# A transformer block on one Trainium2 core: another order for the lead-in's maxima, weight loads and low keys

## The chip, the cores and the metric

The kernel runs on one core of one Trainium2 chip. The metric is the device time of one execution in microseconds (us), as a median over runs. The profile shows one execution of its own. Engines: TensorE (PE; PEld is its weight load), VectorE (DVE), ScalarE (ACT), GpSimd (POOL) and SyncE (SP), whose queue issues nearly all DMA transfers, one after the other.

## What is computed

A layer norm, an attention in which 32 heads share one set of keys and values, and a feed-forward part with the Mish function, whose result passes through a silu and gates the attention's:

```python
B, S, D, H, F = 1, 2048, 512, 32, 1792        # head width Dh = 16
xn = layernorm(x)                              # x: [1, 2048, 512]
q  = (xn @ wq) split into 32 heads             # [32, 2048, 16]
k, v = xn @ wk, xn @ wv                        # [2048, 16] each, for all heads
p  = softmax(q @ k.T * Dh ** -0.5)
s  = (p @ v, heads joined) @ wo
h  = xn @ w1 + b1
g  = silu((h * tanh(softplus(h))) @ w2)
out = x + s * g
```

All of it is in float32; the products that need it are made of two parts, a rounded high part and the rest, the low part.

## The kernel before

The sequence is cut into four chunks of 512 rows, the heads into 32 units (`v`, 8 per chunk) of four heads. For every unit and each of 16 key blocks the main loop computes four tiles of scores (`e_one`, L1010), their exponential on ScalarE (L1015) and the value products (`pv`, L1097). The exponential needs each row's maximum first. So TensorE computes every score a second time the other way round (`m_one`, L1039), and VectorE reduces each 128 x 512 tile to 128 maxima (L1043): 64 tiles for a unit, 32 for each of two sides `a` of the partitions. The maxima run 22 steps (`LEAD`) ahead of the scores; `c_rows` turns a unit's maxima into rows and sends them into the query tile (L1082). Between these lie the projections of the feed-forward part and of the queries, as groups of 12 products into one bank `xps` (`fill`, L112 whole, L116 in halves beside other products). ScalarE empties a group's bank: `hb` (L763) for the first feed-forward layer, `qf` (L708) for queries.

Before the main loop stands the lead-in, at 0 to 99.5 us of the span: loading x, the norm, transposing x (`xp`, L294), the projection to keys and values (`kp`, L335), the first query group, and 88 of the tiles for the maxima: 64 of unit 0, and 12 of each side of unit 1.

- Keys. For chunk 0 the key rows come out on partitions 0 to 63 alone; for the others, half the columns on partitions 0 to 63 and half on 64 to 127. ScalarE copies the high parts to `ks` (`k_high`, L340), VectorE subtracts to the low parts (`k_low`, L169), and DMA carries each half to the other side (`k_move`, L348). A tile of maxima needs all 512 columns of its chunk on its side, so for chunk 0 only side 1 needs a transfer.
- Queries. `qt` (L722) takes 12 small transfers for each of units 0 and 1, in four parts of three: half `p` and side `a`.
- Values. ScalarE copies them out of the bank (`v_copy`, L353), TensorE transposes them (L358), VectorE copies them to `vaug` (L361).
- Weights. A weight block is loaded to one of two raw tiles (`rawws`, `rawwb`, `rawwq`; L495, L497). ScalarE writes its high part (L449), GpSimd its low part (L169); `xtw` and `ws` are such blocks of w1, `wbs` of w2. The raw tile is free for the next load once GpSimd has read it. An engine takes its instructions in order, and SyncE waits at a load until its raw tile is free.
- The order is found when the program is built: a planner in the lead-in has for each engine a list of tasks with estimated durations and picks the one that can start first (`best`, L1337). `m_ready` picks the next tile of the maxima, both sides as a pair; where nothing is ready, TensorE gets a group's products or a product that nobody reads (`keep_warm`, L1317). `landed` (L1202) estimates when a load has arrived, and `arrived` (L427) whether a block may be split.

In the main loop the order is written out by step: units of four steps, with the products of one group among them.

Of the kernel before, what the change touches and what calls it, by code (L numbers as in the profile page):

```python
# [20 lines left out]
P = 128  # L21
# [101 lines left out]
def block_kernel(ctx: ExitStack, tc: tile.TileContext, x, wq, wk, wv, wo, w1, b1, w2, out):  # L123
# [156 lines left out]
    def x_scale(t):  # L280
        x_ = xin[divmod(t, 4)]
        if t % 2 == 0:
            (dve if t < 4 else pool).tensor_scalar(x_, x_, rstd[:, t:t + 1], nbias[:, t:t + 1], op0=ALU.mult, op1=ALU.add)
        else:
            xn_scale(x_, x_, t)
# [64 lines left out]
    def v_copy(c):  # L350
        vt_of[c] = sb.tile([P, C], F32, tag="xr", name=f"vt{c}", bufs=4)[0:32]
        for o, z, _ in sides(c):
            act.activation(vt_of[c][:, z], kp_of[c][o + 32:o + 64, 0:z.stop - z.start], AF.Copy)  # L353

    def v_transpose(c):
        vp = vp_of[c] = ps_v.tile([P, 4, 32], F32, tag="v", name=f"vp{c}")
        for tt in range(4):
            pe.transpose(vp[:, tt], vt_of[c][:, P * tt:P * (tt + 1)], ident[0:32, 0:32])  # L358

    def v_out(c):  # L360
        dve.tensor_copy(vaug[:, 4 * c:4 * c + 4, 0:DH], vp_of[c][:, :, 16:32])  # L361
# [161 lines left out]
    def begin():  # L523
# [16 lines left out]
        else:  # L540
            ps = ps_x.tile([P, 512], F32, tag="x", name="xps")
# [154 lines left out]
    def q_group(c, b):  # L696
        it = item("wq", ("q", b), wq[:, P * b:P * (b + 1)].rearrange("(t p) n -> p t n", p=P))

        def post(ps):
# [12 lines left out]
            for k in range(2):  # L712
# [10 lines left out]
                if first:  # L723
                    lead["qdma"](lambda ps, dmas=dmas: dmas(parts=[(p, a) for p in ps for a in range(2)]))
# [460 lines left out]
    T = {"PE": 11.0, "ACT": 2.0, "DVE": 3.4, "POOL": 5.5, "SP": 3.0}  # L1185
# [16 lines left out]
    def landed(us):  # L1202
        dma_t[0] = max(dma_t[0] + us, now[0] + 2.2)
# [10 lines left out]
    def put_off(g, ps):  # L1214
# [4 lines left out]
        t = task("ACT", 0.69, fn, at=now[0] + 0.35)  # L1219
# [4 lines left out]
    def q_low(fn):  # L1224
        lead["qlow"] = task("DVE", 0.69, fn, at=T["ACT"] + 0.7)

    def q_dma(fn):
        v = len(qready)
        qready[v] = None

        def move(p):
            fn(ps=(p,))
            qready[v] = (qready[v] or ()) + (now[0] + 6 * 0.63 + 2.0,)
        for p in range(2):
            task("SP", 6 * 0.63, lambda p=p: move(p), [lead["moved"] if p + v else lead["qlow"]], prio=1 + p + 2 * v)
# [13 lines left out]
    xat.update({t: landed(DMA_US) for t in range(8, 16)})  # L1249
    warm = ps_v.tile([P, C], F32, tag="v", name="warm")  # L1250
# [12 lines left out]
    for t in range(12, 16):  # L1263
        ss = task("ACT", 0.6, lambda t=t: stats_sum(t), at=xat[t], prio=4)
        st.append(task("ACT", 0.6, lambda t=t: stats_var(t), [ss], prio=4))
    kv_done = None
    for c in range(NC):
# [6 lines left out]
        for t in range(4 * c, 4 * c + 4):  # L1274
            e, us = ("ACT", 0.8) if t % 2 else ("DVE", 0.55) if c == 0 else ("POOL", 0.8)
# [27 lines left out]
        kl = task("DVE", 0.86 if c else 0.68, lambda c=c: k_low(c), [kh])  # L1303

        def mv(c=c):
            k_move(c)
            kready[c] = now[0] + 2.6
# [3 lines left out]
        vc = task("ACT", 0.76 if c else 0.59, lambda c=c: v_copy(c), [kp])  # L1311
        bank("v", 1, k0, [kl, vc])
        vtr = task("PE", 0.5, lambda c=c: v_transpose(c), [vc], fill=c > 0)
        vo = task("DVE", 0.22, lambda c=c: v_out(c), [vtr])
# [9 lines left out]
    pick = [0]  # L1324

    def m_ready(t):
        if min(m_next) >= 2 * LEAD:
            return None
        s = [None, None]
        for v in range(2):  # L1330
            n = got[v]
            if n < 32 and len(qready.get(v) or ()) > n % 8 // 4 and n // 8 in kready:
                s[v] = max(t, qready[v][n % 8 // 4], kready[n // 8], m_ends[(-3, -5)[len(mseq) % 2] if 15 in xp_of else -2])
        pick[0] = int(s[0] is None or s[1] is not None and s[1] + 0.6 < s[0])
# [216 lines left out]
```

## Time and profile before

| | us |
|---|---|
| median of 3 runs (lowest, highest) | 1596.12 (1593.78, 1597.36) |
| the profiled execution | 1591.68 |
| its span, first to last instruction | 1589.9 |
| first product for maxima; first score | 29.19; 99.73 |
| TensorE busy in 110 to 200 us | 90.00 of 90 |
| TensorE busy in 20 to 100 us, eight windows of 10 | 8.21, 9.63, 5.98, 9.53, 9.21, 9.70, 7.03, 8.91 |

The profile has busy times per engine, windows of the span with the clock that TensorE was granted (1.00 is full), and timelines: start, length, engine, line, what was written from what, and in brackets how long the engine stood idle before it and what ended that. In a window the numbers after the length are busy us. Buffer numbers are left out there (`xtw<-rawws`), while the order of a program, below, keeps them (`rawws_537`).

### The profile page before, as it was taken

What the parts mean: (1) busy time and instruction counts of PE and PEld (TensorE: products, weight loads), DVE (VectorE), ACT (ScalarE), POOL (GpSimd) and SP (SyncE); (2) the same over time, 40 slices, a digit from 0 to 9 for tenths busy, and PEclk for the clock granted to TensorE, in tenths of its full rate; (3) what the DMA queues carried; (4) which work ended last, traced back from release to release, by engine and by line L of the source; (5) the groups of instructions that cost most, each with busy time, mean ns of one, the idle gap of its engine ahead of it and who ended that gap; (6) DMA issues with size and microseconds to landing.
All of it is one profiled execution on the core that took longest, in us unless ns stands there. A gap on an engine that the chain in (4) does not pass through costs nothing.

```text
span 1589.9 us, 31336 instructions
## 1 busy us (share of the span) xinstructions
PE 1567.2 (99%) x11680; PEld 881.2 (55%) x11680; DVE 1335.8 (84%) x2282; ACT 1297.4 (82%) x2512; POOL 638.9 (40%) x671
## 2 busy tenths in 40 slices
PE   8889999999999999999999999999999999999998
PEld 5445655655555565565555556556655555655643
DVE  6888888888988988888898988888889999888821
ACT  5469889878899778887988888797788978888796
POOL 4677438527368210531524523153152323315021
PEclk9899999999999999999999999999999999999999
DMA  6322125114152213103104230322321213031200
GB/s 185 122 90 87 31 74 164 58 53 158 33 177 63 77 58 111 57 24 104 55 18 150 65 104 26 102 69 70 110 58 49 88 58 115 15 97 32 74 21 27
DMA packets 74887, 124.42 MB, mean 78 GB/s; under 512 B 21536, under 2 KB 37184, under 8 KB 74736
## 3 DMA queue, kind: packets, MB, share of 16 engines
q1 hardware_dynamic: 74664, 122.41, 24.6%
q8 instruction: 93, 1.52, 0.4%
q14 instruction: 58, 0.48, 0.1%
q10 hardware_dynamic: 72, 0.01, 0.0%
HBM read 74.52 MB, written 26.21 MB: 63 GB/s over the span
## 4 chain that ended last, share of the span: by engine, by line
PE 94%; ACT 2%; DVE 1%; DMA 1%; POOL 1%; issue 0%; SPq 0%; DVEq 0%; POOLq 0%; ACTq 0%
PE xps L116 42%; PE pv L1097 31%; PE m L1039 11%; PE e L1010 6%; PE xps L112 1%; ACT pts L1015 1%; DVE mb L1043 1%; PE warm L1252 1%; PE warm L1321 0%; DMA rawwb<-in_dram 0%; PE wop L112 0%; PE xp L294 0%; SPq L722 0%; DMA rawws<-in_dram 0%; DMA rawwq<-in_dram 0%
## 5 line engine op out<-in xcount | busy, mean ns | idle before, releaser
L1043 DVE TENSOR_REDUCE mb<-m 128x1 f32<-128x512 f32 x2048 | 1266.2, 682 | 175.3 <-PE m L1039 152.5
L1015 ACT ACTIVATE pts<-e 128x512 f32<-128x512 f32 x2042 | 1062.4, 606 | 217.4 <-PE e L1010 147.3
L1039 PE MATMUL m<-ks,qt 48*128 48x512 f32 (+1 forms) x2048 | 842.4, 427 | 1.0 <-DMA ks<-ks 0.7
L1010 PE MATMUL e<-qt,ks 64*128 64x512 f32 x2048 | 747.2, 407 | 2.0 <-ACT pts L1015 1.7
L1097 PE MATMUL pv<-pts,vaug 128*32 128x512 f32 x4084 | 531.0, 603 | 0.0
L1039 PEld LDWEIGHTS m<-ks,qt 48*128 48x128 f32 (+1 forms) x2048 | 367.8, 186 | 106.4 <-DVE mb L1043 54.3
L1010 PEld LDWEIGHTS e<-qt,ks 64*128 64x128 f32 x2048 | 372.4, 186 | 28.6 <-ACT pts L1015 18.1
L116 PE MATMUL xps<-wbs,act 64*128 64x512 f32 x1248 | 315.2, 397 | 0.0
L116 PE MATMUL xps<-xt,ws 64*128 64x512 f32 x1122 | 311.4, 410 | 0.2 <-ACT pts L1015 0.2
L116 PEld LDWEIGHTS xps<-xt,ws 64*128 64x128 f32 x1122 | 193.3, 185 | 182.2 <-ACT pts L1015 121.3
L116 PEld LDWEIGHTS xps<-wbs,act 64*128 64x128 f32 x1248 | 226.5, 185 | 65.6 <-ACT pts L1015 33.5
L1097 PEld LDWEIGHTS pv<-pts,vaug 128*32 128x32 f32 x4084 | 87.8, 108 | 150.4 <-issue 142.4
L169 POOL TENSOR_TENSOR hb<-hb,t 128x512 f32<-128x512 f32 x56 | 72.2, 1289 | 152.7 <-ACT t L782 72.6
L179 POOL TENSOR_SCALAR t<-t 128x512 f32<-128x512 f32 x56 | 34.4, 615 | 171.6 <-ACT t L769 171.5
L116 PE MATMUL xps<-xt,wq 64*128 64x512 f32 x336 | 93.0, 409 | 0.0
L116 PEld LDWEIGHTS xps<-xt,wq 64*128 64x128 f32 x336 | 57.9, 185 | 55.0 <-ACT pts L1015 37.7
L169 POOL TENSOR_TENSOR oc<-oc,sc 128x512 f32<-128x512 f32 (+1 forms) x16 | 20.6, 1288 | 147.6 <-DMA qt<-qh 47.0
L116 PE MATMUL xps<-wbs,ot_all 64*128 64x512 f32 x288 | 79.4, 408 | 0.0
L116 PEld LDWEIGHTS xps<-wbs,ot_all 64*128 64x128 f32 x288 | 49.5, 184 | 47.1 <-ACT pts L1015 29.3
L169 POOL TENSOR_TENSOR act<-hb,act 128x512 fp32r<-128x512 f32 x56 | 72.2, 1290 | 4.7
L169 POOL TENSOR_TENSOR hb<-hb,u 128x512 f32<-128x512 f32 x56 | 72.3, 1291 | 4.4
L169 POOL TENSOR_TENSOR u<-u,t 128x512 f32<-128x512 f32 x56 | 72.0, 1285 | 4.7
(141 smaller groups left out, 885.9 us busy)
## 6 DMA issues: line engine op xcount, KB each, us to landing
wbs<-w SPq DMA_DIRECT2D x38, 512.0 KB
ws<-w SPq DMA_DIRECT2D x32, 512.0 KB
qt<-qh SPq DMA_DIRECT2D x256, 32.0 KB
w<-wbs SPq DMA_DIRECT2D x14, 512.0 KB
w<-ws SPq DMA_DIRECT2D x14, 512.0 KB
wq<-wq SPq DMA_DIRECT2D x14, 512.0 KB
rawws<-in_dram SPq DMA_DIRECT2D x24, 256.0 KB
wbs<-wo SPq DMA_DIRECT2D x12, 512.0 KB
```

Source lines behind the costliest of these rows:

```text
L112: self.pe.matmul(ps, self.lhs(), self.rhs(), start=(self.k == 0), stop=(self.k == self.tot - 1))
L116: i = self.pe.matmul(ps, self.lhs()[o], self.rhs()[o], start=(self.k == 0 and self.halves == 0), stop=(self.k == self.tot - 1 and self.hal ...
L169: eng.tensor_tensor(out=o, in0=a, in1=b, op=op)
L179: pool.tensor_scalar(o, o, lim, 0.0, op0=ALU.min, op1=ALU.max)
L1010: pe.matmul(e, ks[o:o + 64, P * k:P * (k + 1)], q[o:o + 64, p], start=True, stop=True)
L1015: x = act.activation(dst, e, AF.Exp, scale=0.25)
L1039: pe.matmul(m, q[o, p, P * t:P * (t + 1)], ks[o, C * kb:C * (kb + 1)], start=True, stop=True)
L1043: return dve.reduce_max(out=mb_of[v][:, kb, z:z + 1], in_=m, axis=AX.X)
L1097: pe.matmul(o[32 * j:32 * j + 32], vaug[:, k], pt, start=(k == 0), stop=(k == 15))
L1252: pe.matmul(warm, qts[0][:, 0, 0:P], qts[0][:, 0], start=True, stop=True)
```

## The change

It touches the lead-in alone.

- `m_ready` no longer demands both sides as a pair: tiles of side 0, whose chunk-0 keys need no transfer, may go first (up to four), and side 1 follows. A query group's transfers are four tasks of three instead of two of six.
- Products that nobody reads go to one tile that is kept (`lead["w"]`) in place of a new one each.
- `landed` counts SyncE's time: each load takes 0.45 us of it, so an estimated arrival moves back when SyncE is busy. `arrived` lets fewer weight blocks of w1 ahead (two more than the evacuated groups after 50 us), a split is held while a GpSimd task is about to come (`soon`), and the evacuation of a group without queries ready is expected 2.9 us later.
- For chunks 1 to 3 ScalarE copies all 128 partitions of the key and value bank in one instruction, TensorE transposes twice in place of four times, and ScalarE in place of VectorE writes `vaug`. For chunks 1 and 2 GpSimd subtracts the low keys from that copy; chunks 0 and 3 stay on VectorE.
- The scaling of x in chunk 3 goes wholly to ScalarE (two of four tiles were GpSimd's). The sums of squares of chunk 3 wait for chunk 0's key copy.

```diff
     def x_scale(t):
-        if t % 2 == 0:
+        if t % 2 == 0 and t < 12:
...
     def k_low(c):
         for o, z, t in sides(c):
-            sub(dve, ks[o:o + 16, t], kp_of[c][o:o + 16, 0:z.stop - z.start], f(ks[o:o + 16, t]))
+            if c in (0, 3):
+                sub(dve, ks[o:o + 16, t], kp_of[c][o:o + 16, 0:z.stop - z.start], f(ks[o:o + 16, t]))
+            else:
+                sub(pool, ks[o:o + 16, t], vt_of[c][o:o + 16, 0:C // 2], f(ks[o:o + 16, t]))
...
     def v_copy(c):
-        vt_of[c] = sb.tile([P, C], F32, tag="xr", name=f"vt{c}", bufs=4)[0:32]
-        for o, z, _ in sides(c):
-            act.activation(vt_of[c][:, z], kp_of[c][o + 32:o + 64, 0:z.stop - z.start], AF.Copy)
+        vt_of[c] = sb.tile([P, C], F32, tag="xr", name=f"vt{c}", bufs=4)
+        if c == 0:
+            act.activation(vt_of[c][0:32], kp_of[c][32:64], AF.Copy)
+        else:
+            act.activation(vt_of[c][:, 0:C // 2], kp_of[c][:, 0:C // 2], AF.Copy)
...
     def v_out(c):
-        dve.tensor_copy(vaug[:, 4 * c:4 * c + 4, 0:DH], vp_of[c][:, :, 16:32])
+        if c == 0:
+            dve.tensor_copy(vaug[:, 0:4, 0:DH], vp_of[c][:, :, 16:32])
+        else:
+            act.activation(vaug[:, 4 * c:4 * c + 4, 0:DH].rearrange("p (h j) n -> p h j n", h=2),
+                           vp_of[c][:, :, :, 48:64].rearrange("p j h n -> p h j n"), AF.Copy)
...
     def arrived(tag):
-        if taken(tag, k) or lead and tag == "ws" and k > len(hb_hist) - NHB + 4:
+        if taken(tag, k) or tag == "ws" and k < 12 and k > len(hb_hist) - NHB + (4 if lead and now[0] < 50 else 2):
             return False
...
     def landed(us):
-        dma_t[0] = max(dma_t[0] + us, now[0] + 2.2)
+        T["SP"] = max(T["SP"], now[0]) + 0.45
+        dma_t[0] = max(dma_t[0] + us, T["SP"] + 2.2)
         return dma_t[0]
...
-        t = task("ACT", 0.69, fn, at=now[0] + 0.35)
+        t = task("ACT", 0.69, fn, at=now[0] + (0.35 if qready else 2.9))
...
-        for p in range(2):
-            task("SP", 6 * 0.63, lambda p=p: move(p), [lead["moved"] if p + v else lead["qlow"]], prio=1 + p + 2 * v)
+        for p, a in ((0, 0), (0, 1), (1, 0), (1, 1)):
+            task("SP", 3 * 0.63, lambda p=p, a=a: move(p, a), [lead["moved"] if p + v else lead["qlow"]], prio=1 + 2 * p + a + 4 * v)
...
     def keep_warm():
-        ps, tag = (ps_m, "m") if waiting else (ps_x, "x")
-        w = ps.tile([P, C], F32, tag=tag, name="warm")
+        if waiting:
+            w = ps_m.tile([P, C], F32, tag="m", name="warm")
+        else:
+            w = lead["w"] = lead.get("w") or ps_x.tile([P, C], F32, tag="x", name="warm")
...
     def m_ready(t):
...
+        if m_next[0] == m_next[1]:
+            free = m_ends[(-3, -5)[len(mseq) % 2] if 15 in xp_of else -2]
+            s = [max(free, *(ready(v, got[v], a) for a in range(2))) if got[v] < 32 else 1e9 for v in range(2)]
+            v = int(s[1] + 0.6 < s[0])
+            r.append((s[v], (0, 1), (v, got[v])))
+        else:
+            e = mseq[m_next[1]]
+            r.append((max(ready(*e, 1), m_ends[-3]), (1,), e))
+        if m_next[0] < 4:
+            r.append((max(ready(0, got[0], 0), m_ends[-3]) + 0.3, (0,), (0, got[0])))
+        z, pick[0], pick[1] = min(r, key=lambda z: z[0])
```

What this does to the order. ScalarE of before, around the third chunk's key copy (the `ks<-kp` row): `sq` and `sv` are sums for the last x tile, `xtw`, `wq` and `wbs` the splits of weight blocks, `vt` the copy of values.

```order
L240 ACTIVATE sq_532,nms<-xin_3_146 128x512
L449 ACTIVATE wq_534<-rawwq_444 128x512
L244 ACTIVATE sv_548,mvs<-xin_3_146,nms 128x512
L449 ACTIVATE wbs<-rawwb_198 128x512
L449 ACTIVATE xtw<-rawws_537 128x512
L340 ACTIVATE ks<-kp_545 48x256 x2
L353 ACTIVATE vt_591<-kp_545 32x256 x2
```

The same place on ScalarE now; `rawws_250` is the load that stands ahead of all query transfers on SyncE (`rawws_254` before), `rstd` the norm of the last chunk.

```order
L240 ACTIVATE sq_520,nms<-xin_3_146 128x512
L244 ACTIVATE sv_533,mvs<-xin_3_146,nms 128x512
L257 ACTIVATE rstd<-ve 128x4
L258 ACTIVATE rstd<-rstd 128x4
L463 ACTIVATE xtw<-rawws_250 128x512
L340 ACTIVATE ks<-kp_524 48x256 x2
L358 ACTIVATE vt_575<-kp_524 128x256
```

Two splits have moved behind the key copy, and the one that is left ahead of it is of an earlier load.

SyncE of before, around the last chunk's key transfer (`ks<-ks`); `xtk` is the transposed x sent to memory, and after the transfer come the weight loads ahead of the rows of the maxima (`qt_77<-cr_983`).

```order
L495 DMA rawws_735<-in_dram 128x4x128
L497 DMA rawwb_778<-in_dram 128x512
L348 DMA ks<-ks 48x256 x2
L495 DMA rawws_837<-in_dram 128x4x128
L495 DMA rawws_877<-in_dram 128x4x128
L495 DMA rawws_914<-in_dram 128x4x128
L495 DMA rawws_966<-in_dram 128x4x128
L1082 DMA qt_77<-cr_983 2x8x32 x4
```

The same place on SyncE now:

```order
L509 DMA rawws_680<-in_dram 128x4x128
L947 DMA xtk_673<-xf_1_612 128x1024
L511 DMA rawwb_693<-in_dram 128x512
L509 DMA rawws_753<-in_dram 128x4x128
L351 DMA ks<-ks 48x256 x2
L511 DMA rawwb_791<-in_dram 128x512
L509 DMA rawws_802<-in_dram 128x4x128
L509 DMA rawws_898<-in_dram 128x4x128
L509 DMA rawws_940<-in_dram 128x4x128
L1097 DMA qt_77<-cr_952 2x8x32 x4
```

Four loads stand between the key transfer and the rows in both, one of them now for `wbs`. The load ahead of the key transfer, `rawws_753`, waits for the raw tile of `rawws_680`, which GpSimd reads.

GpSimd of before, around the last of the splits that came ahead of that key transfer (`wbs<-rawwb_727`); `t`, `u` and `hb` are steps of Mish.

```order
L169 TENSOR_TENSOR wbs<-rawwb_609,wbs 128x512
L169 TENSOR_TENSOR ws_732<-rawws_691,ws_732 128x512
L169 TENSOR_TENSOR wbs<-rawwb_727,wbs 128x512
L169 TENSOR_TENSOR hb_0_611<-hb_0_611,t_0_654 128x512
L164 TENSOR_SCALAR act_0_800<-hb_0_611 128x512
```

GpSimd now, up to the split of `rawws_680`:

```order
L169 TENSOR_TENSOR xtw<-rawws_637,xtw 128x512
L169 TENSOR_TENSOR wbs<-rawwb_654,wbs 128x512
L179 TENSOR_SCALAR t_0_734<-t_0_734 128x512
L787 TENSOR_SCALAR u_0_735<-t_0_734 128x512
L169 TENSOR_TENSOR u_0_735<-u_0_735,t_0_734 128x512
L169 TENSOR_TENSOR hb_0_726<-hb_0_726,u_0_735 128x512
L169 TENSOR_TENSOR xtw<-rawws_680,xtw 128x512
```

The first group's four operations stand ahead of the split that frees the raw tile.

More of the change, by code (lines that the diff above doesn't have):

```diff
@@ L723, in post @@
                 if first:
[L724 removed]
+                    lead["qdma"](dmas)
                 else:
@@ L1184, in block_kernel @@
     vdone = [0]
-    T = {"PE": 11.0, "ACT": 2.0, "DVE": 3.4, "POOL": 5.5, "SP": 3.0}
+    T = {"PE": 11.0, "ACT": 2.0, "DVE": 3.4, "POOL": 5.5, "SP": 0.2}
     dma_t = [3.3]
@@ L1274, in block_kernel @@
         for t in range(4 * c, 4 * c + 4):
-            e, us = ("ACT", 0.8) if t % 2 else ("DVE", 0.55) if c == 0 else ("POOL", 0.8)
+            e, us = ("ACT", 0.8) if t % 2 or c == 3 else ("DVE", 0.55) if c == 0 else ("POOL", 0.8)
             sc = task(e, us, lambda t=t: x_scale(t), [nrm], prio=c and 1)
@@ L1343, in best, with soon @@
         return found
+    def soon(k, t):
+        return all(d.end is not None and d.end < t + 2.0 or d.end is None and d.deps and all(x.end is not None for x in d.deps)
+                   for d in k.deps)
     begun = [0]
@@ L1410, in block_kernel @@
         elif k == "J":
-            tag = next((g for g in ("wq", "ws", "wb") if arrived(g) and busy[0] + E0 < s + (4.5 if g == "ws" else 0.5)), None)
+            tag = next((g for g in ("wq", "ws", "wb") if not any(soon(k, s) for k in plan["POOL"]) and arrived(g) and busy[0] + E0 < s + (4.5 if g == "ws" else 0.5)), None)
             n = ran[0]
```

77 lines of the change are left out of this document (47 added, 30 removed).

## The prediction

> **What bounds the kernel now.** The page comes first. The span is the profiled execution's 1591.68 us less 1.78 us around it, and TensorE is busy in 99% of it.
>
> ```profile
> span 1589.9 us, 31336 instructions
> PE 1567.2 (99%) x11680; PEld 881.2 (55%) x11680; DVE 1335.8 (84%) x2282; ACT 1297.4 (82%) x2512; POOL 638.9 (40%) x671
> ```
>
> That average hides the stage that the change touches, so the next view is the table of windows (length, then busy us of PE, PEld, DVE, ACT, POOL; granted clock, DMA share, GB/s).
>
> ```profile
> 40.00:50.00 10.00, 5.98 (x30) 2.70 (x26) 6.34 (x11) 5.08 (x13) 4.20 (x5) 1.00 0.57 188
> 50.00:60.00 10.00, 9.53 (x32) 5.32 (x33) 6.32 (x12) 4.95 (x11) 8.71 (x14) 0.56 0.21 57
> 80.00:90.00 10.00, 7.03 (x29) 4.29 (x28) 7.57 (x16) 2.93 (x5) 5.06 (x6) 0.94 0.19 53
> 110.00:200.00 90.00, 90.00 (x695) 51.03 (x695) 77.50 (x133) 79.29 (x154) 54.76 (x55) 1.00 0.23 74
> ```
>
> From 110 us on TensorE never rests, so nothing there can shrink unless its instructions change, and they do not: the last 7,502 of some 7,700 rows of TensorE's order are the same in both kernels. The change can only move the moment at which the main loop begins. The timeline of TensorE gives that moment (the first score product) and the first product for the maxima:
>
> ```profile
> 29.19 0.89 PE L1039 MATMUL m<-ks,qt 64*128 64x512 f32 x2
> 99.73 0.39 PE L1010 MATMUL e<-qt,ks 64*128 64x512 f32 x1
> ```
>
> Between them VectorE must reduce 84 of the 88 maxima of the lead-in; the last four run into the loop. Its timeline, first and last rows:
>
> ```profile
> 29.72 2.68 DVE L1043 TENSOR_REDUCE mb<-m 128x1 f32<-128x512 f32 x4 [1.70 <-PE m L1039]
> ...
> 99.45 3.08 DVE L1043 TENSOR_REDUCE mb<-m 128x1 f32<-128x512 f32 x5 [0.74 <-PE m L1039]
> ```
>
> A reduction costs 0.62 us (3.08 / 5). 84 of them are 52 us of the 69.7 us between 29.72 and 99.45. The rest is other work and waiting, which the list of waits of this stretch names (us in total, times, longest):
>
> ```profile
> ACT xtw L449 <- DMA rawws<-in_dram: 17.3, 4, 4.9
> DVE mb L1043 <- PE m L1039: 12.4, 15, 1.9
> ```
>
> VectorE waits for products, TensorE for banks that ScalarE empties, and ScalarE for weights whose load was issued late. The largest case stands in the timelines of ScalarE, SyncE and TensorE: ScalarE sits 4.06 us on a load issued only at 43.11, behind the query transfers in SyncE's order; TensorE then idles 3.92 us, and its clock falls to 0.56 in the next window.
>
> ```profile
> 46.45 0.63 ACT L449 ACTIVATE xtw<-rawws 128x512 fp32r<-128x512 f32 x1 [4.06 <-DMA rawws<-in_dram]
> 43.11 0.53 SPq L495 DMA_DIRECT2D rawws<-in_dram  x1
> 50.47 0.50 PE L1321 MATMUL warm<-qt 128*128 128x512 f32 x1 [3.92 <-ACT hb L763]
> ```
>
> **The change part by part, as VectorE time before the loop.**
>
> *The maxima start earlier.* The untransferred side goes first, the 0.87 us of three feed-forward products ahead of it go (28.32 to 29.19), and ScalarE no longer puts a sum of squares ahead of the first key copy.
>
> ```profile
> 24.13 0.66 PE L294 MATMUL xp<-ident,pts 128*128 128x128 f32 x4 [0.66 <-POOL pts L283]
> 27.27 0.43 PE L358 MATMUL vp<-ident,vt 32*128 32x32 f32 x4 [1.13 <-DVE ks L169]
> 28.32 0.94 PE L112 MATMUL xps<-xt,xtw 128*128 128x512 f32 x3
> ```
>
> With the second block's norm now ahead of the query copy on ScalarE, the 0.66 us wait goes too, and with the earlier key copy the 1.13 us: 0.66 + 1.13 + 0.87 = 2.7 us. **-2.7** (-1 if the query transfers are the next thing late).
>
> *Work leaves VectorE.* Two of three low-key subtractions and three copies of values go.
>
> ```profile
> 35.20 0.87 DVE L169 TENSOR_TENSOR ks<-kp,ks 16x256 fp32r<-16x256 f32 x2 [0.16 <-ACT vt L353]
> 38.50 0.21 DVE L361 COPY vaug<-vp 128x64 f32<-128x64 f32 x1
> ```
>
> 2 x 0.87 + 3 x 0.2 = **-2.3**. The copies land on ScalarE, which has 5 us in 10 free. The subtractions land on GpSimd in a form the trace lacks; its own subtractions bound it:
>
> ```profile
> L169 POOL TENSOR_TENSOR xtw<-rawws,xtw 128x512 fp32r<-128x512 f32 x8 | 10.2, 1276 | 17.1 <-ACT xtw L449 12.5 <-DMA rawwb<-in_dram 3.4 <-PE m L1039 1.2
> L169 POOL TENSOR_TENSOR wk<-wkv,wk 128x64 fp32r<-128x64 f32 x4 | 1.5, 370 | 0.0
> ```
>
> Between 0.37 and 1.28 us each; by length (256 of 64 to 512 elements) 0.76, which I take.
>
> *The stall at 46 us.* The weight split that ScalarE meets there is now of a tile loaded before the query transfers, so its wait goes, and with it these rows of VectorE, the half-speed clock's included (0.48 four times, between 56.16 and 61.47):
>
> ```profile
> 48.55 0.86 DVE L169 TENSOR_TENSOR ks<-kp,ks 16x256 fp32r<-16x256 f32 x2 [2.98 <-ACT vt L353]
> 52.09 1.29 DVE L1043 TENSOR_REDUCE mb<-m 128x1 f32<-128x512 f32 x2 [1.36 <-PE m L1039]
> 54.39 1.29 DVE L1043 TENSOR_REDUCE mb<-m 128x1 f32<-128x512 f32 x2 [0.89 <-PE m L1039]
> 56.16 1.29 DVE L1043 TENSOR_REDUCE mb<-m 128x1 f32<-128x512 f32 x2 [0.48 <-PE m L1039]
> ...
> 61.47 6.07 DVE L1043 TENSOR_REDUCE mb<-m 128x1 f32<-128x512 f32 x10 [0.48 <-PE m L1039]
> ```
>
> 2.98 + 1.36 + 0.89 + 4 x 0.48 = **-7.15**. What is late next there is the second key chunk: its first copy starts about 2 us earlier, near 31.6, plus 0.75 and 0.4 of copies, 2 x 0.76 on GpSimd, and 2.95 from issue to first use (below, 69.53 to 72.48) makes 37.2; the sixteen reductions of the first chunk end near 29.72 - 2.7 + 16 x 0.62 = 36.9. With the queue's own spacing I add **+1.0** (0 to 2).
>
> *A new wait on SyncE.* The transfer of the last key chunk now stands behind a weight load whose raw tile is free only after GpSimd has split the load before, and that split stands behind the four operations of the first feed-forward group. SyncE waits in order, so the keys wait as well. Rows of before, GpSimd's chain and the old transfer with its use:
>
> ```profile
> 54.78 0.61 POOL L179 TENSOR_SCALAR t<-t 128x512 f32<-128x512 f32 x1 [0.52 <-ACT t L769]
> ...
> 58.76 1.27 POOL L169 TENSOR_TENSOR xtw<-rawws,xtw 128x512 fp32r<-128x512 f32 x1
> 69.53 1.16 SPq L348 DMA_DIRECT2D ks<-ks x2
> 72.48 0.82 PE L1039 MATMUL m<-ks,qt 64*128 64x512 f32 x4 [0.16 <-DMA ks<-ks]
> ```
>
> From the chain's first operation to the split's end is 58.76 + 1.27 - 54.78 = 5.25 us. On the new clock the 44 reductions ahead of the last low keys end at 27.0 + 44 x 0.62 + 1.0 = 55.3. The first feed-forward group finishes next to them; with 1.3 us for its two ScalarE steps the chain starts near 55.8 and the load goes at 61.0. The keys leave at 61.5 and are usable at 64.4, their product is there at 64.9. VectorE has 0.87 + 8 x 0.62 = 5.8 us of other work and runs dry at 61.1. **+4.0** (0 if that group is early; 6 if one more 1.3 us split and a slower load come between).
>
> *The end of the lead-in.* Five waits of VectorE, each behind ScalarE's waits for weights (the load issues took SyncE 16.44 us, with the rows of the maxima queued behind them):
>
> ```profile
> 83.82 2.48 DVE L1043 TENSOR_REDUCE mb<-m 128x1 f32<-128x512 f32 x4 [0.49 <-PE m L1039]
> 88.47 2.48 DVE L1043 TENSOR_REDUCE mb<-m 128x1 f32<-128x512 f32 x4 [1.88 <-PE m L1039]
> 92.14 2.48 DVE L1043 TENSOR_REDUCE mb<-m 128x1 f32<-128x512 f32 x4 [1.07 <-PE m L1039]
> 96.23 2.48 DVE L1043 TENSOR_REDUCE mb<-m 128x1 f32<-128x512 f32 x4 [1.61 <-PE m L1039]
> 77.70 16.44 SPq L495 DMA_DIRECT2D rawws<-in_dram  x4
> 94.23 2.76 SPq L1082 DMA_DIRECT2D qt<-cr  x4
> ```
>
> With 0.74 at 99.45 that is 5.8 us. Splits now follow the group's evacuation, but the products still share one bank, so I keep 2.0 of it (0 to 5.8): **-3.8**. The rows of the maxima again stand behind a load that waits for GpSimd. Counting its queue from 61.0 (eleven operations of 1.28, six of 0.62, and 3 us of starts that wait for ScalarE) the load goes near 82 and the first score, 5.5 us after the rows as before (94.23 to 99.73), near 88.
>
> **Sum:** -2.7 - 2.3 - 7.15 + 1.0 + 4.0 - 3.8 = -10.95, so the loop starts at 88.5 instead of 99.5, level with the 88 that SyncE allows. The loop carries it whole: it then has three more feed-forward products in half form, under others. 1591.68 becomes 1580.7. That run was 4.44 us under the median of 1596.12, so the median becomes 1585.1, called 1585. About 0.2%, 3.2 us, is what a measurement of this kernel can tell from no change.
>
> **The rivals.** *The new stall brings the half clock back* (0.20).
>
> ```profile
> 81.69 1.66 PE L112 MATMUL xps<-xt,xtw 128*128 128x512 f32 x6 [1.53 <-ACT hb L763]
> ```
>
> Before, 3.92 us idle at once was followed by 0.56; the 3.0 us of the window 80 to 90, the longest piece 1.53, by 0.94. The new stall leaves TensorE some 2.4 us (from the products queued ahead, done near 62, to 64.4), between the two. If the clock falls, the rows at 52.09 to 61.47 price it: 1.36 + 0.89 + 1.92 = 4.2 us, giving 1589. The Trainium skill, "TensorE: Matmul & The Clock Gate", section "Part 1: The HAM clock gate", says that an idle window of some 3.4 us halves the clock: by that rule a 2.4 us gap is safe and 1585 stands, and one 1 us longer is not. The 3.92 us row agrees; a gap between 1.5 and 3.9 us is not in this trace.
>
> *GpSimd's queue sets the start* (0.12). It had 5.8 and 1.3 us free in the two windows from 40 to 60, but the forecast packs it from 56 to 82, and the rows of the maxima wait at its end. Each of five weight splits there that waits out a load as at 43.11 to 46.45 (3.3 us) instead of finding it landed slips the start. Three such are 10 us: 1595, no change. For it: a load may only start when the raw tile is released. Against: most have two tiles of lead.
>
> *Slower* (0.05).
>
> ```profile
> 51.26 0.80 PE L1039 MATMUL m<-ks,qt 64*128 64x512 f32 x2
> 51.99 1.65 PE L112 MATMUL xps<-xt,xtw 128*128 128x512 f32 x3
> ```
>
> If idle gaps recur and the clock stays at half from 61 us to the loop, TensorE becomes the bound: two products took 0.80 and a three-product piece 1.65 us at half clock, so four and six are 4.9 us where VectorE needs 2.5. Nine such sets of four remain: 9 x 2.4 = 21.6 us, less the 2 us of waits already counted, against the 10.95 won: 8.7 us slower, 1605. It decides from the seventh set on (10.95 + 2 + 3.2 over 2.4). The window 80 to 90, idle in pieces and at 0.94, speaks against it.
>
> **How the numbers follow.** The forecast has 0.63, half clock 0.20, GpSimd 0.12, slower 0.05. Without the new SyncE wait the sum is -15, 1581; the half clock with 3 us of the other upper bounds gives 1592. From 1580.5 to 1592 leaves out the last two rivals. Faster: 0.63 + 0.20 = 0.83; same 0.12; slower 0.05.
>
> **What would show it.** In the changed profile: first reduction near 27; no ScalarE wait on weights near 42 and the clock 1.00 from 50 to 60; a VectorE gap of about 4 us near 61 ended by the key transfer; the first score near 88; from there on the same rows 11 us earlier. A first score after 95, a clock under 0.9 for 10 us, or a loop longer than before's 1490 us would make the prediction wrong.

## The result, and the profile after

The changed kernel takes 1587.27 us (median of 5 runs, 1585.09 to 1588.99), against 1595.5 us before in the same runs: ratio 0.9949, 95% interval 0.9934 to 0.9963, so about 8 us faster. Forecast were 1585 and a range of 1580.5 to 1592. The profiled execution took 1585.09 us; its page:

```profile
span 1583.3 us, 31336 instructions
PE 1563.0 (99%) x11682; PEld 880.2 (56%) x11682; DVE 1333.4 (84%) x2275; ACT 1297.2 (82%) x2511; POOL 638.5 (40%) x672
```

The span is 6.6 us shorter. The windows of after (length; busy PE, PEld, DVE, ACT, POOL; clock, DMA share, GB/s) show where:

```profile
40.00:50.00 10.00, 10.00 (x52) 5.55 (x50) 9.92 (x17) 7.21 (x18) 5.02 (x5) 1.00 0.30 77
50.00:60.00 10.00, 9.17 (x42) 4.87 (x42) 9.94 (x18) 5.45 (x11) 7.66 (x8) 1.00 0.51 179
60.00:70.00 10.00, 5.73 (x18) 3.44 (x19) 4.83 (x9) 2.99 (x5) 6.40 (x7) 0.83 0.32 89
80.00:90.00 10.00, 7.57 (x29) 4.48 (x31) 7.07 (x13) 3.60 (x6) 5.53 (x5) 0.90 0.14 40
```

The hole of 40 to 50 us and the half clock behind it (0.56 from 50 to 60) are filled: VectorE is busy 9.92 and 9.94 of 10. A new hole stands at 60 to 70, with TensorE at 5.73 and the clock at 0.83, and the end of the lead-in is hardly denser than it was (7.57 from 80 to 90, before 7.03). TensorE's timeline gives both ends of the stretch:

```profile
23.85 0.73 PE L1054 MATMUL m<-ks,qt 64*128 64x512 f32 x2
91.15 0.56 PE L1025 MATMUL e<-qt,ks 64*128 64x512 f32 x1
```

The first product for the maxima comes at 23.85 instead of 29.19, the first score at 91.15 instead of 99.73: 8.6 us earlier. VectorE's timeline between them, the rows with a wait from 24 us on but those under 0.3 us:

```profile
24.39 2.01 DVE L1058 TENSOR_REDUCE mb<-m 128x1 f32<-128x512 f32 x3 [1.00 <-PE m L1054]
26.71 0.69 DVE L1058 TENSOR_REDUCE mb<-m 128x1 f32<-128x512 f32 x1 [0.31 <-PE m L1054]
27.71 2.48 DVE L1058 TENSOR_REDUCE mb<-m 128x1 f32<-128x512 f32 x4 [0.31 <-PE m L1054]
31.55 5.16 DVE L1058 TENSOR_REDUCE mb<-m 128x1 f32<-128x512 f32 x8 [1.35 <-PE m L1054]
37.32 2.48 DVE L1058 TENSOR_REDUCE mb<-m 128x1 f32<-128x512 f32 x4 [0.62 <-PE m L1054]
...
64.09 2.48 DVE L1058 TENSOR_REDUCE mb<-m 128x1 f32<-128x512 f32 x4 [3.80 <-PE m L1054]
67.94 2.48 DVE L1058 TENSOR_REDUCE mb<-m 128x1 f32<-128x512 f32 x4 [1.38 <-PE m L1054]
71.16 4.87 DVE L1058 TENSOR_REDUCE mb<-m 128x1 f32<-128x512 f32 x8 [0.73 <-PE m L1054]
...
76.70 2.48 DVE L1058 TENSOR_REDUCE mb<-m 128x1 f32<-128x512 f32 x4 [0.37 <-PE m L1054]
...
87.27 2.48 DVE L1058 TENSOR_REDUCE mb<-m 128x1 f32<-128x512 f32 x4 [2.69 <-PE m L1054]
90.53 4.87 DVE L1058 TENSOR_REDUCE mb<-m 128x1 f32<-128x512 f32 x8 [0.78 <-PE m L1054]
```

The 3.80 is the forecast wait for the last key chunk. How it comes about stands in the timelines of GpSimd (the first group's chain, to the split that frees the raw tile), SyncE and TensorE:

```profile
54.63 0.61 POOL L179 TENSOR_SCALAR t<-t 128x512 f32<-128x512 f32 x1 [0.63 <-ACT t L784]
...
58.62 1.28 POOL L169 TENSOR_TENSOR xtw<-rawws,xtw 128x512 fp32r<-128x512 f32 x1
59.93 0.38 SPq L509 DMA_DIRECT2D rawws<-in_dram  x1
60.40 1.15 SPq L351 DMA_DIRECT2D ks<-ks  x2
63.58 0.90 PE L1054 MATMUL m<-ks,qt 64*128 64x512 f32 x4 [3.63 <-DMA ks<-ks]
64.41 2.93 PE L112 MATMUL xps<-xt,wq 128*128 128x512 f32 x6
```

The split ends at 59.90, the load goes at 59.93, the keys behind it at 60.40, their product at 63.58. The six products that follow take 2.93 us; six of the kind took 1.66 at full clock. ScalarE still waits 3.29 us for a load, at 50.76, but TensorE stays busy meanwhile. The end of the lead-in, on ScalarE and TensorE:

```profile
82.25 3.20 ACTq L1097 DMA_DIRECT2D qt<-cr  x4
85.56 0.69 ACT L778 ACTIVATE hb<-xps,b1c 128x512 f32<-128x512 f32 x1 [4.83 <-DMA qt<-cr]
86.31 0.50 PE L1348 MATMUL warm<-qt 128*128 128x512 f32 x1 [2.43 <-ACT hb L778]
...
87.40 2.37 PE L1348 MATMUL warm<-qt 128*128 128x512 f32 x6
```

ScalarE issues four transfers of rows of maxima, 3.20 us, and only then empties the last group's bank. TensorE stands 2.43 us for it, and then six products that nobody reads take 2.37.

### The profile page after: what moved, and what is told of

The parts are those of the page before. It is cut to its first block, busy times and chain, and to the rows that moved or that the text cites. A ratio compares the mean times of both kernels' runs of the same rounds, so it can differ in the third digit from the quotient of the medians.

```text
span 1583.3 us, 31336 instructions
## 1 busy us (share of the span) xinstructions
PE 1563.0 (99%) x11682; PEld 880.2 (56%) x11682; DVE 1333.4 (84%) x2275; ACT 1297.2 (82%) x2511; POOL 638.5 (40%) x672
## 4 chain that ended last, share of the span: by engine, by line
PE 93%; ACT 2%; POOL 2%; DVE 1%; DMA 1%; issue 0%; SPq 0%; ACTq 0%; DVEq 0%; POOLq 0%
PE xps L116 41%; PE pv L1112 31%; PE m L1054 12%; PE e L1025 6%; PE xps L112 1%; ACT pts L1030 1%; DMA rawwb<-in_dram 1%; PE warm L1269 1%; DVE mb L1058 0%; POOL wbs L169 0%; PE wop L112 0%; PE warm L1348 0%; DMA ks<-ks 0%; PE kp L335 0%; POOL u L169 0%
```

## The experiments

The theory after the profile had four points: (1) the arrival estimates remove the stall at 46 us, (2) the kept tile brings the start forward, which the forecast had at nothing, (3) the weight load ahead of the last keys costs what the new stall shows, (4) the last evacuation behind ScalarE's transfers costs the end. "Whole" below is the changed kernel; the kernel before was timed beside each, at 1594.6 to 1595.2 us. Times are medians, while ratios go by all runs, so that the two can differ by 2 us. The interval of a ratio is some 2 us to either side, and so a difference between two of these kernels is known to about 3 us. Each profile is of one execution; that of before, 1591.68 us, was a fast one.

**Whole, fresh tiles.** The kept tile alone is undone; on each engine the instructions stand as in whole.

```diff
     def keep_warm():
-        if waiting:
-            w = ps_m.tile([P, C], F32, tag="m", name="warm")
-        else:
-            w = lead["w"] = lead.get("w") or ps_x.tile([P, C], F32, tag="x", name="warm")
+        ps, tag = (ps_m, "m") if waiting else (ps_x, "x")
+        w = ps.tile([P, C], F32, tag=tag, name="warm")
```

> The changed kernel with the unread products on a new tile each again, nothing else; every engine's order stays. Theory: a new tile in the one bank makes each of these products wait for the one before (0.55 us apart, where on one tile they are 0.26 apart), so the eight ahead of the first query group take 2.3 to 2.7 us longer, the first reduction goes from 24.4 to about 27 us, and everything after it shifts: about 1590, first score near 94. Rival: the different pace of these eight comes from the clock or the run and not from the tile, or the wait for the last key chunk swallows the shift: 1587, first score near 91.

1590.55 us, ratio 0.998 (0.9969 to 0.9991). TensorE's timeline, the end of the lead-in:

```profile
90.59 4.74 PE L1346 MATMUL warm<-qt 128*128 128x512 f32 x6
```

The first reduction comes at 26.57, 2.2 us later than in whole, and the first score at 96.71, 5.6 later: the six products take 4.74 us where one tile took 2.37. A part of that is the clock (0.66 from 90 to 100): at full clock six on fresh tiles would take 3.3, by the 0.55 us from one to the next that eight of them show (last section). The kept tile is worth 3.3 us by the medians and 4.9 by the ratios.

**Before, one tile.** The same edit alone, put into the kernel before (the diff turned round, and the tile given up where a group begins).

```diff
     def begin():
...
+            lead.pop("w", None)
```

> The kernel before with the unread products on one kept tile, nothing else; every engine's order stays. Theory: the first reduction goes from 29.7 to about 27 us and all that follows with it: 2.7 us less, about 1592.8. Rival: the wait for the weight load at 42 us hangs on loads and not on the products, and the gain is lost there: 1595.5.

1589.86 us, ratio 0.9973 (0.9961 to 0.9985). The first reduction comes at 27.61 instead of 29.72, as from the other side, while the stall at 46 stays (clock 0.50 from 50 to 60). The gain is more than was expected: 4.8 us by the medians, against a start that moved 2.1. In the profiles the first score comes only 1.3 us earlier (98.42), so the rest stays unexplained; that the one of before was a fast execution is a part of it.

**Before, arrivals.** The estimates of arrivals alone.

```diff
     def arrived(tag):
-        if taken(tag, k) or lead and tag == "ws" and k > len(hb_hist) - NHB + 4:
+        if taken(tag, k) or tag == "ws" and k < 12 and k > len(hb_hist) - NHB + (4 if lead and now[0] < 50 else 2):
...
-    T = {"PE": 11.0, "ACT": 2.0, "DVE": 3.4, "POOL": 5.5, "SP": 3.0}
+    T = {"PE": 11.0, "ACT": 2.0, "DVE": 3.4, "POOL": 5.5, "SP": 0.2}
...
     def landed(us):
-        dma_t[0] = max(dma_t[0] + us, now[0] + 2.2)
+        T["SP"] = max(T["SP"], now[0]) + 0.45
+        dma_t[0] = max(dma_t[0] + us, T["SP"] + 2.2)
...
+    T["SP"] = 15.0
```

> The kernel before with the planner's new estimate of arrivals alone (SyncE's time per load, fewer blocks ahead). Theory: ScalarE's 4 us wait at 42 us, TensorE's 3.9 us gap and the half clock from 50 to 60 go, which were priced at 7.15 us of VectorE; a new wait may take 1 to 3 us of it: 1588 to 1592, clock 1.00 from 50 to 60. Rival: the stall moves to another load of the same queue and the half clock comes back: 1594 or more.

1593.13 us, ratio 0.9992 (0.9982 to 1.0003): no change that can be told. Yet the stall is gone, as its windows and the end of its lead-in on TensorE show:

```profile
50.00:60.00 10.00, 9.93 (x50) 5.12 (x49) 9.91 (x18) 4.64 (x11) 5.34 (x7) 1.00 0.60 196
...
90.00:100.00 10.00, 9.77 (x28) 5.23 (x27) 5.08 (x9) 0.48 (x1) 2.55 (x3) 0.55 0.27 89
```

```profile
87.60 0.50 PE L1323 MATMUL warm<-qt 128*128 128x512 f32 x1 [2.54 <-ACT hb L763]
...
88.69 4.99 PE L1323 MATMUL warm<-qt 128*128 128x512 f32 x6
...
99.06 0.40 PE L1010 MATMUL e<-qt,ks 64*128 64x512 f32 x1
```

The maxima are transposed 7.7 us earlier than before (83.21, before 90.87), and the first score comes 0.7 earlier. What was won is lost from 85 on: an idle 2.54 us, half clock (0.55 from 90 to 100), and unread products on fresh tiles, 4.99 us for six. That made the next experiment.

**Before, arrivals and one tile.** Both edits, and nothing of the rest.

> The kernel before with two of the four parts of the change: the arrival of weights by SyncE's time, and the kept tile for unread products. Alone the first gave 1593.1 (no change) and the second 1589.9, against 1594.6 before. Theory (the two need each other: without the 46-us stall the last group's unread products run at half clock on fresh tiles, 4.99 us for six, and give the gain back): here these six take 1.7 to 2.4 us, the first reduction starts near 27.6, the first score product near 92 to 94, the time is 1586.5 to 1589, most of what the whole change brings. Rival 1 (the parts add): 1588.5 with the first score near 97. Rival 2 (the tail takes the gain back whatever the unread products do, through the last group's evacuation and the rows of maxima): first score after 97, 1590 or more.

1586.96 us, ratio 0.9945 (0.9932 to 0.9957): as fast as whole. TensorE after the same wait:

```profile
84.74 0.50 PE L1326 MATMUL warm<-qt 128*128 128x512 f32 x1 [2.45 <-ACT hb L764]
...
85.83 1.66 PE L1326 MATMUL warm<-qt 128*128 128x512 f32 x6
```

The same six take 1.66 us, and the first score comes at 90.64. Alone the edits are worth 0.08% and 0.27%, together 0.55%. That is 0.2% more than their sum, and the intervals leave 0.2% open, so that each gives the other its gain is likely and not shown. The profiles have a second cause beside the tile: from the transposition of the maxima to the first score it is 10.20 us here (from 80.44) and 15.85 with fresh tiles. Of this 5.65 us the fresh tiles explain 1.6 (six at full clock, 3.3 against 1.66) to 2.1 (at half clock, 4.99 against 2.93); most of the rest is the half clock, which one execution had after a wait of 2.54 us and the other, after 2.45, had not. What is shown is that these two parts bring as much as the whole; since taking work off VectorE should win something too, another part probably costs something.

**Whole, pairs first.** Both sides as a pair from the first tile on, as before the change.

```diff
-        if m_next[0] < 4:
+        if False:
```

> The whole change, but with the first key positions taken in pairs again, so that the side without transferred keys does not go first. Theory (this part is worth the wait for the transferred keys only, which the first reductions no longer show much of: the kept tile alone brought the start forward by 2.1 of its 5.3 us): the first reduction starts near 26.5 instead of 24.4, 1 to 2 us are lost, 1588 to 1589.5. Rival (the stall on the last key chunk at 64 us swallows what is lost at the start, since VectorE runs dry there whatever came before): VectorE's wait there shrinks from 3.8 to 2 us or less and the time stays at 1587.3 within 0.5.

1582.03 us, ratio 0.9915 (0.9902 to 0.9929): 5.2 us faster than whole. Neither theory had that; both had the start alone in view. The first reduction does come 1.2 us later, at 25.60. GpSimd, SyncE and VectorE around the last keys:

```profile
54.01 1.27 POOL L169 TENSOR_TENSOR xtw<-rawws,xtw 128x512 fp32r<-128x512 f32 x1
55.31 0.38 SPq L509 DMA_DIRECT2D rawws<-in_dram  x1
...
56.98 1.16 SPq L351 DMA_DIRECT2D ks<-ks  x2
60.92 2.48 DVE L1058 TENSOR_REDUCE mb<-m 128x1 f32<-128x512 f32 x4 [1.54 <-PE m L1054]
```

Where the untransferred side goes first, its tiles stand ahead of the first feed-forward products, which come at 35.31 on TensorE instead of 23.51. Their bank is emptied at 53.19 instead of 47.48, GpSimd's chain follows, and the raw tile is free at 59.90 instead of 55.28. The keys leave at 60.40 instead of 56.98. The part that wins 1.2 us at the start makes 2.3 of the 3.8 us of the stall at 64; a wait of 1.54 us stays, since with pairs a `wbs` load that GpSimd also holds up goes just ahead of the keys (56.56).

**Whole, one load in an idle tile.** The weight load ahead of the last keys gets a tile that nobody uses in the lead-in, so it no longer waits for GpSimd. On each engine the instructions stand as in whole.

```diff
-            r = sb.tile([P, D], F32, tag="raw", name=f"raw{tag}{n}", bufs=RAWS)
+            k = {4: "y1"}.get(n) if lead and tag == "ws" else None
+            r = sb.tile([P, D], F32, tag=k or "raw", name=f"raw{tag}{n}", bufs=1 if k else RAWS)
```

> The changed kernel with one weight load, the one ahead of the last key chunk's transfer, into a tile that is idle in the lead-in, so that it waits for no raw tile; every engine's order stays. Theory: SyncE then sends the keys when VectorE has made them (about 56 us instead of 60.4), the gap of 3.8 us on VectorE at 64 us falls under 0.5, the clock stays at 1.00 from 60 to 70, and the first score comes 4 to 5 us earlier: about 1582.5. Rival: the end of the lead-in gives it back, since the rows of the maxima wait for further loads and for the last group's evacuation: gain under 1 us, 1586.5 or more.

1581.76 us, ratio 0.9925 (0.9908 to 0.9943). SyncE and the windows:

```profile
55.26 1.16 SPq L351 DMA_DIRECT2D ks<-ks  x2
```

```profile
60.00:70.00 10.00, 8.85 (x39) 4.74 (x37) 9.29 (x16) 3.07 (x6) 9.67 (x10) 1.00 0.18 52
```

The keys leave 5.1 us earlier, the hole and the half clock of 60 to 70 are gone, and 5.5 us are won by the medians, 3.8 by the ratios, whose intervals just touch. The profiled execution is the fastest of the six, and no window of it is under full clock.

**Whole, pairs and one idle tile.** The lines of the last two edits together.

> The whole change with the first key positions in pairs (alone 1582.0), and with one weight load in an idle tile, so that it no longer stands ahead of the last key chunk waiting for GpSimd (alone 1581.8). Theory A (pairs win because the first feed-forward group's products come ahead of the maxima, GpSimd is done with that group 5 us earlier, the raw tile is free at 55.2 instead of 59.9 and the keys leave at 57.0 instead of 60.4): then the two cures are for one thing, the second adds little, and the start that is 1.2 us later stays: 1581 to 1583. Theory B (pairs win in another place): the two add, 1576 to 1578.

1581.99 us, ratio 0.9924 (0.9911 to 0.9938): as with pairs alone. But the edit did not do what was meant. It gives the idle tile to the fifth load of a w1 block. In whole that one stands ahead of the last keys; with pairs only four do, and the fifth comes behind them. GpSimd and SyncE:

```profile
54.88 1.27 POOL L169 TENSOR_TENSOR xtw<-rawws,xtw 128x512 fp32r<-128x512 f32 x1
56.18 0.38 SPq L510 DMA_DIRECT2D rawws<-in_dram  x1
...
57.85 1.16 SPq L351 DMA_DIRECT2D ks<-ks  x2
```

The load ahead of the keys, the fourth, still goes when GpSimd has ended the split before it, then a `wbs` load at 57.43, then the keys, no earlier than with pairs alone. So the time agrees with theory A, but neither theory was tested, and whether the two cures add is open. What the run shows is that freeing a load behind the keys brings nothing that can be told.

**Whole, four loads in idle tiles.** The three loads that stand ahead of the rows of the maxima on SyncE get idle tiles too.

```diff
-            k = {4: "y1"}.get(n) if lead and tag == "ws" else None
+            k = {4: "y1", 5: "y2", 6: "y3", 7: "y1"}.get(n) if lead and tag == "ws" else None
```

> The whole change, with four of the weight loads (the one that waits near 60 us and the three that wait from 65 to 83 us on SyncE) put into tiles that lie idle in the lead-in, so that no weight load on SyncE waits for GpSimd. One such load alone brought 1581.8. Theory (the rows of maxima stand behind these loads, so that they leave late and with them the last group's evacuation on ScalarE): the three issues of 17.4 us go to under 3 us, the rows leave as soon as the maxima are there, the wait of 3.6 us of the last evacuation shrinks below 1 us, the first score comes at 82 to 83.5 instead of 84.9, the time is 1579.5 to 1581. Rival (the rows wait for the maxima themselves and the loads only fill that time): rows sent at the same 79 us, first score 84.5 to 85, time as with one load, 1581.8 within 0.7.

1582.56 us, ratio 0.9927 (0.9914 to 0.9939): nothing more than with one. SyncE, then TensorE:

```profile
60.47 2.48 SPq L510 DMA_DIRECT2D rawws<-in_dram  x3
77.06 2.79 SPq L1098 DMA_DIRECT2D qt<-cr  x4
```

```profile
81.09 0.79 PE L1349 MATMUL warm<-qt 128*128 128x512 f32 x1 [2.45 <-ACT hb L779]
...
82.96 2.93 PE L1349 MATMUL warm<-qt 128*128 128x512 f32 x6
```

The three loads go in 2.48 us instead of 17.6, and the rows still leave when VectorE has the maxima (their transposition is at 76.78). In whole they left at 82.25 and 82.86, with the transposition at 82.02: the loads cost the rows under 1 us there. The last evacuation is where it was, behind ScalarE's transfers.

**Whole, four idle tiles, rows on SyncE.** Of the eight transfers of rows, ScalarE issues two instead of four.

```diff
-                    (act if lead and b % 2 else sp).dma_start(
+                    (act if lead and b == 3 else sp).dma_start(
```

> The run with four loads in idle tiles, and of the eight transfers of rows of maxima two instead of four on ScalarE's queue, six on SyncE's. Theory (the last group's evacuation stands behind ScalarE's four issues, 3.2 us, and TensorE idles 2.4 us for it and then loses its clock): its start comes 1.5 us earlier, TensorE's wait for it falls below 1 us, the first score comes 1 to 2 us earlier than with the four loads alone, 1578.5 to 1580.5. Rival (the first score waits for the rows of maxima, and two more issues on SyncE put them later): the first score stays or comes up to 1 us later, 1581 to 1582.5.

1580.69 us, ratio 0.9906 (0.9892 to 0.992), 1.9 under the run without it, with intervals that overlap. ScalarE, then TensorE:

```profile
79.08 1.89 ACTq L1098 DMA_DIRECT2D qt<-cr  x2
```

```profile
81.82 0.50 PE L1349 MATMUL warm<-qt 128*128 128x512 f32 x1 [1.12 <-ACT hb L779]
...
82.92 1.66 PE L1349 MATMUL warm<-qt 128*128 128x512 f32 x6
```

TensorE's wait falls from 2.45 to 1.12 us, and from the transposition of the maxima (78.85) to the first score (85.33) it is 6.5 us, against 7.8 in the run with one idle tile (77.07 to 84.86), where the clock held as well. The 1.3 us between them are the shorter wait: by the stage point 4 stands, while the times leave it open.

**Whole, pairs, four idle tiles, rows on SyncE.** All of it, as a best version.

> The whole change with pairs, four loads in idle tiles and six of the eight rows of maxima on SyncE (without the pairs 1580.7). Theory A of the run with one idle tile: 1580 to 1582. Theory B: 1575 to 1577. In both the wait of TensorE for the last evacuation is near 1.1 us instead of 2.4.

1578.74 us, ratio 0.9904 (0.9889 to 0.992), 8.5 us under whole and the lowest median of all, though it can't be told from the run without pairs (0.9906). Here too the four loads with idle tiles all stand behind the last keys; the load ahead of them still waits for GpSimd (56.48), and the keys leave at 58.15. So this run does not decide between the theories either, into neither of whose ranges it falls.

**Whole, low keys on VectorE.** The fourth part undone in place.

```diff
-                sub(pool, ks[o:o + 16, t], vt_of[c][o:o + 16, 0:C // 2], f(ks[o:o + 16, t]))
+                sub(dve, ks[o:o + 16, t], vt_of[c][o:o + 16, 0:C // 2], f(ks[o:o + 16, t]))
...
-            act.activation(vaug[:, 4 * c:4 * c + 4, 0:DH].rearrange("p (h j) n -> p h j n", h=2),
-                           vp_of[c][:, :, :, 48:64].rearrange("p j h n -> p h j n"), AF.Copy)
+            dve.tensor_copy(vaug[:, 4 * c:4 * c + 4, 0:DH].rearrange("p (h j) n -> p h j n", h=2),
+                            vp_of[c][:, :, :, 48:64].rearrange("p j h n -> p h j n"))
```

> The whole change, but the two low-key subtractions and the three copies of values stand on VectorE again, at the same places. Theory (VectorE's time ahead of the loop is what counts, work that leaves it is won whole): 2 x 0.87 + 3 x 0.2 = 2.3 us are lost, the first score comes near 93.5, 1589.5. Rival (the end of VectorE's wait for the last key chunk is set by GpSimd and SyncE, so that the wait of 3.8 us swallows what comes ahead of it): that wait shrinks to some 2 us, the first score stays near 91 to 92, 1587 to 1588.

1589.37 us, ratio 0.9969 (0.9956 to 0.9983), 2.1 us over whole, with intervals that overlap. VectorE at the last keys:

```profile
66.61 2.48 DVE L1058 TENSOR_REDUCE mb<-m 128x1 f32<-128x512 f32 x4 [4.00 <-PE m L1054]
```

The wait did not shrink but moved 2.5 us with the rest (4.00 at 66.61, 3.80 at 64.09): the group whose chain GpSimd must finish is itself paced by VectorE. Its bank is emptied at 55.55 instead of 53.19, and on the way there TensorE waits for a reduction of VectorE (0.88 us, at 44.06). The rival falls: up to the last keys, work that leaves VectorE is won whole. The first score comes 1.7 us later (92.89).

**Whole, a bridge over the stall.** Twelve products that nobody reads keep TensorE busy while it waits for the last keys; the wait stays.

```diff
+        if (v, n, a) == (0, 24, 0):
+            for _ in range(12):
+                pe.matmul(m, qts[2][:, 0, 0:P], qts[2][:, 0], start=True, stop=True)
         pe.matmul(m, q[o, p, P * t:P * (t + 1)], ks[o, C * kb:C * (kb + 1)], start=True, stop=True)
```

> The whole change, with twelve products that nobody reads put ahead of the first product of the last key chunk, into the same bank, so that TensorE is busy for some 3.1 of the 3.6 us in which it waits for the keys. The wait itself stays. Theory (the half clock after the wait is a cost of its own): clock 1.00 from 60 to 70 instead of 0.83, the six products after it take 1.7 instead of 2.9 us, VectorE's wait of 1.38 us behind them goes, the first score comes 1.2 to 1.6 us earlier, 1585.5 to 1586.3. Rival (the half clock is hidden, since the later waits end by SyncE's and ScalarE's work): the wait of 1.38 us goes but returns in the waits after it, 1587.3 within 0.5.

1586.75 us, ratio 0.9952 (0.9937 to 0.9967): by time it cannot be told from whole. TensorE:

```profile
26.07 0.50 PE L1057 MATMUL m<-ks,qt 64*128 64x512 f32 x1 [0.79 <-DMA ks<-ks]
26.50 1.12 PE L335 MATMUL kp<-xf,wkf 128*64 128x256 f32 x4
...
65.57 2.90 PE L1056 MATMUL m<-qt 128*128 128x512 f32 x12
69.44 0.81 PE L1057 MATMUL m<-ks,qt 64*128 64x512 f32 x4 [0.97 <-DMA ks<-ks]
70.18 1.67 PE L112 MATMUL xps<-xt,wq 128*128 128x512 f32 x6
```

The stage does what the theory says: the six products take 1.67 instead of 2.93 us, and from the first product with the last keys to the first score it is 26.29 us (69.44 to 95.73) instead of 27.57. But this execution had lost its clock at 26 us already (four `kp` products in 1.12 us instead of 0.65), which whole's profile had not, so 1.3 us for the half clock rest on the stage alone.

## Why the prediction was right, and where it failed

Right: the sign, the stall at 46 us with its half clock as the thing that goes, and the new wait on SyncE with its cause. VectorE ran dry at 60.28 (forecast 61.1) and had its product at 64.09 (64.9). Term by term:

- *Start, -2.7.* It was -5.3 (29.72 to 24.39). The forecast gave the kept tile nothing; it alone is 2.1 to 2.2, from both sides.
- *The second key chunk, +1.0.* Its wait is 0.62 us, at 37.32. But the forecast ran the sixteen reductions of the first chunk one behind the other, and these wait 2.0 us more (0.31, 0.31 and 1.35). So the better start was lost again by 60 us, and the forecast was right there by luck.
- *Work off VectorE, -2.3.* In the run that undoes it 2.5 us at the last keys, 1.7 at the first score and 2.1 in time. The estimate of 0.76 us for GpSimd's subtraction held, in the timeline of after:

```profile
30.85 1.51 POOL L169 TENSOR_TENSOR ks<-vt,ks 16x256 fp32r<-16x256 f32 x2 [3.53 <-ACT vt L358]
```

- *The stall, -7.15.* Gone in every kernel with the arrival estimates. But by itself that is worth nothing that can be told (ratio 0.9992), and 0.28% beside the kept tile: the sum counted it as won, and not that the late end, half clock and fresh tiles could take it back 30 us later.
- *The new wait, +4.0.* 3.80 us. Taking it away wins 3.8 to 5.5 us: the wait, and the half clock behind it. What the forecast did not see is that the untransferred side, booked under gains, causes 2.3 us of it.
- *The end, -3.8.* This is the step that failed. The waits from 67.94 on are 1.38 + 0.73 + 0.37 + 2.69 + 0.78 = 5.95 us against 5.8 before. The first of them stands behind the six products at half clock and belongs to that rival; without it 4.6 are left, so 1.2 us were won and not 3.8. The forecast had the waits go with the weight splits. The largest, 2.69, is the last evacuation behind ScalarE's four transfers, which the change left alone, and the run with two of them brought it down. "The rows again stand behind a load that waits for GpSimd" was true of the order and near nothing in time: under 1 us in whole, and no gain when the loads were freed.
- *The loop, 0.* From the first score to the start of the last ScalarE instruction (at 1572.89, before at 1579.48) it is 1481.7 us instead of 1479.8: 2.0 us are given back. It is 1479.9 with one tile alone and 1481.1 to 1483.0 in each kernel with the arrival estimates, so it goes with the order that these set up. The change does not touch the lead-in alone: `arrived` no longer asks for `lead`, so that the first twelve w1 blocks are held back in the loop as well. Whether that costs the 2 us was not tested. Up to the end of the span the loop is 1492.2 us, before 1490.2; a loop longer than before's was one of the prediction's own signs against it.

Added up as the forecast was, these are -5.3 - 2.3 + 2.0 + 0.6 - 7.15 + 3.8 + 1.4 - 1.2 = -8.2 us, against the forecast's -10.95; the wait that was at 99.45 ends at 90.53, 8.9 us earlier, and what is missing are waits of before under 0.4 us that went too. For the profiled execution the sum gave 1580.7, and it took 1585.09, 4.4 us more: some 2.4 from the lead-in, 2.0 from the loop. That the median came within 2.3 us of the forecast is luck in part: the forecast set it 4.4 us over the profiled execution, as it was before, and here it lies 2.2 over.

Of the rivals, the half clock came back in part: 0.83 from 60 to 70, 1.3 to 1.4 us instead of the 4.2 priced. The gap that decides was 3.63 us where 2.4 was forecast, since the products queued ahead were done at 59.95, not near 62. Reading the rule of the Trainium skill, "TensorE: Matmul & The Clock Gate", section "Part 1: The HAM clock gate", as a length of gap that is safe or not was half of it: the same section says that the window runs free of the program. The runs agree in so far as the same gap had two outcomes (last section); no run here shows the window itself. GpSimd's queue as the bound of the start is ruled out by the run with four idle tiles, and the slower case needed a clock that stayed low, which it did not: the mean of 0.83 from 60 to 70, under the 0.9 that the prediction named as a sign against it, is one spell of half clock over the six products at 64.41, and the next window is back at full.

## What to carry to other kernels

Price a removed stall by what is late after it, to the end of the stage: here a stall that had cost VectorE 7 us went, and no change could be told, since the end of the stage took it back. A part that starts one chain earlier starts another later; follow the one that is pushed back (feed-forward products, GpSimd, raw tile, SyncE, keys) before booking the gain. Look at what stands behind a transfer in its issuing engine's queue: giving the load ahead of the keys a tile of its own brought about as much as the best single edit of the change. And look in the trace whether an edit hit what it was meant for: the load picked by its number stood ahead of the keys in one order and behind them in another.

## What the hardware showed

Products that nobody reads, each on a fresh tile of the bank ring, ran 0.55 us apart at full clock (eight in 4.39 us), on one kept tile 0.26 us apart (eight in 2.07). With the clock low, six took 4.99 (0.55 from 90 to 100) and 2.93 us (0.66 from 80 to 90, four idle tiles).

The half clock did not follow from the length of one gap. After the same wait for the last evacuation, of 2.42 to 2.46 us, six products on one tile took 1.65 or 1.66 us in three kernels (one idle tile; arrivals and one tile; low keys on VectorE), 2.93 in two (four idle tiles; pairs and one idle tile), and between in three (2.37 in whole; pairs first; the bridge). After 3.4 to 3.9 us it fell each time, in five kernels. But it also fell after 0.79 and 0.81 us (the bridge; rows on SyncE, at 26 us), and at the same place not after 0.77 and 0.84 (low keys on VectorE; one idle tile). That may be part of the scatter between executions of one kernel (3.9 us in whole), which was not tested.
